# A two-part kernel on one core: block transposes by VectorE and a trip through DRAM in place of TensorE's transposes, with queries cut 64 + 4 x 128

## The chip, the core and the metric

The kernel runs on one NeuronCore of one Trainium2 chip. Its engines run side by side, each with its own queue of instructions worked through in order: TensorE (PE, with its weight loads as PEld), VectorE (DVE), ScalarE (ACT), GpSimd (POOL), and SyncE (SP), which here issues every DMA. The transfers themselves are carried out row by row by 16 DMA engines. The metric is the device time of one execution in microseconds.

## The reference, cut to what matters

```python
# q, k, v: (8 batches, 8 heads, 576, 64), f: (8, 8, 576)
scores = scale * q @ k^T
cum = cumsum(log(clip(f, 1e-4, 1)))                     # over the 576 positions
scores = where(causal, scores + cum[:, None] - cum[None, :], -1e9)
attn = exp(scores - max(scores)); attn /= sum(attn) + 1e-9
x = (attn @ v) transposed and reshaped to (4608, 512)   # one row per token
h = x @ w_in                                            # (4608, 2048)
out = maximum(0.01 * h, h) @ w_out                      # (4608, 512)
```

Everything is float32. The kernel gets this accuracy by splitting a number into a high part (float32r) and a remainder, and by multiplying the parts.

## The kernel before, in words

There are 64 attention tasks, one per head, and behind them one feed-forward layer over 4608 tokens. Batches 3 to 7 are taken whole, which gives 40 tasks with all 576 queries. For batches 0 to 2 the first 256 queries are done in a short "early" phase at the start (`early_load`, `early_scores`, `early_values`), so that their 24 tasks at the end do only queries 256 to 575 (`c0 = 2`). The feed-forward layer runs over groups of 256 tokens; it is cut into small pieces (`ffn`, `second`), which `fill` puts between the attention's pieces, as many per step as the tokens that are ready allow.

One turn of the loop at L694 is a round. In round t the kernel:

- loads q and k of task t + 1 (`load`, L235): each is fetched twice, into partitions 0 to 63 and into 64 to 127, by two DMAs of 64 rows; for each second task the values v of two heads as well;
- computes the scores of task t (`scores`, L403) in five chunks of 128, 128, 128, 96 and 96 queries, each against all keys up to its own end: two matmuls (L420), a mask, scale and row maximum on VectorE (L425), an exponential with its row sum on ScalarE (L431);
- turns the exponentials of task t - 1 (`transposes`, L436): TensorE multiplies each block of 128 keys with an identity (L447) into PSUM, ScalarE writes the high part `ph` (L460) and VectorE the remainder `pl` (L462);
- multiplies them with v (`values`, L474, matmuls on L489) and, when both heads of a pair are done, scales by the inverse row sums. These are turned on TensorE, written to DRAM as `inv` (L515) and read back broadcast over 64 partitions as `rb` (L521, two DMAs of 64 rows); `normalise` (L523) multiplies and writes to `xd` in DRAM, where the feed-forward layer fetches its tokens (L543);
- splits q, k and v of task t + 1 into their parts (`split`, L380), with the high part of q copied to the other half of `s2` by a DMA (L392).

The order within each engine's queue follows a scheduler that works from these calls; within the SP queue a DMA waits for its inputs and its destination, and everything behind it waits too. Eight DMA semaphores are used in turn, so that a DMA also waits for the one eight places ahead of it. The tiles `qraw` and `kraw` have one buffer each: the loads of task t + 2 wait until `split` of task t + 1 has read them.

The lines that the change touches:

Of the kernel before, what the change touches and what calls it, by code (L numbers as in the profile page):

```python
# [23 lines left out]
B2 = 7  # L24
# [9 lines left out]
ZE = (("z0", "z1", "z2", "z3"), ("vm", "s2b", "m2b", "s2a"))  # L34
# [9 lines left out]
def forgetting_attention_ffn(ctx, tc, qT, kT, v4, vr, f, w_in, w_out, out):  # L44
# [15 lines left out]
    STEP = (P + REST) // 2  # L60
    ST = [*range(0, (NFULL - 1) * P + 1, P)]
    ST.append(ST[-1] + STEP)
# [5 lines left out]
    PST = S - P  # L68
    PT0 = NFULL * PST + STEP
    PTW = PT0 + P  # L70
# [7 lines left out]
    def rows(i):  # L78
        return P if i < NFULL - 1 else STEP

    def width(i):
        return ST[i] + rows(i)

# [6 lines left out]

    def segments(n):

        at = n * P
        while at < (n + 1) * P:
            b, lo, hi = next(x for x in reversed(blocks) if place[x[:2]] <= at)
            skip = at - place[b, lo]
            m = min(hi - lo - skip, (n + 1) * P - at)
            yield at - n * P, b * S + lo + skip, m
            at += m

# [31 lines left out]
    inv = dram.tile([NHEAD // 2, 2, S], F32, name="inv")  # L132
    dec_k, dec_q = (dram.tile([NHEAD, 2, S], F32, name=n) for n in ("dec_k", "dec_q"))

    dry = one.tile([P, 1], F32, name="dry")
# [56 lines left out]
    def decays():  # L192
# [42 lines left out]
    def load(t):  # L235
# [4 lines left out]
        for name, src, lo in (("q", qT, a), ("k", kT, 0)):  # L240
            x = h[name] = one.tile([P, S], F32, tag=f"{name}raw", name=f"{name}raw_{t}")
            for o in range(2):
                nc.sync.dma_start(x[o * D:(o + 1) * D, lo:n], src[s][:, lo:n])
        if s % 2 == 0:
# [4 lines left out]
            pairs[s // 2, c0] = dict(vm=vm)  # L249

    early = {}

    def early_load(b, g):

        e = early[b, g] = {}
        x = e["qk"] = one.tile([P, 2, T], F32, tag="b2", name=f"qk_{b}_{g}", bufs=B2)
# [4 lines left out]
        v = e["v"] = one.tile([P, 2, T // P, D], F32, tag="b2", name=f"ve_{b}_{g}", bufs=B2)  # L261
        nc.sync.dma_start(v, v4[b * HPB // 2 + g][:, :, :T // P])

    def early_split(b, g, mx, sm):
# [13 lines left out]
        for i in range(2):  # L278
            n, at = width(i), i * P
# [7 lines left out]
        for i in range(2):  # L287
            n, at = width(i), i * P
            for o in range(2):
                c = 2 * o + i  # L290
                z = e[c] = one.tile([P, n], F32, tag=ZE[g % 2][c], name=f"ze_{b}_{g}_{c}")
# [8 lines left out]
    def early_scores(b, g):  # L300
# [5 lines left out]
        else:  # L306
            for o in range(2):
                s = b * HPB + 2 * g + o
                for i in range(2):
                    n, c = width(i), 2 * o + i  # L310
# [28 lines left out]
    def early_values(b, g):  # L339
        e = early[b, g]  # L340
        out = psum.tile([P, 512], F32, tag="tr", name=f"ave_{b}_{g}")
        for o in range(2):
# [5 lines left out]
            pt = one.tile([P, 3 * P], F32, tag=("z4", "m2a")[o], name=f"pte_{b}_{g}_{o}")  # L348
# [15 lines left out]
    def fix():  # L364

        for x in "ab":
# [4 lines left out]
            y = fixed["sum" + x] = one.tile([P, NCH, 2], F32, tag="sum" + x, name=f"fixed_sum{x}")  # L371
            nc.gpsimd.memset(y, 1.0)
        for i in range(NFULL - 1, NCH):
            z = fixed[f"z{i}"] = one.tile([P, (i + 1) * P], F32, tag=f"z{i}", name=f"fixed_z{i}")
            nc.gpsimd.memset(z, 0.0)
        vs = fixed["vs"] = one.tile([P, 2, NCH, 2 * D], F32R, tag="vs", name="fixed_vs")
        vm = fixed["vm"] = one.tile([P, 2, NCH, D], F32, tag="vm", name="fixed_vm")
        nc.gpsimd.memset(vm[:, :, NFULL], 0.0)

    def split(t):  # L380
# [12 lines left out]
        nc.sync.dma_start(s2[2:4, a:n].bitcast(F32), dec_q[s][:, a:n])  # L393
        nc.sync.dma_start(m2[:2, :n].bitcast(F32), dec_k[s][:, :n])
        minus(s1[:D, a:n], h["q"][:D, a:n], s1[:D, a:n].bitcast(F32))
        minus(m2[D:, :n], h["k"][D:, :n], m1[D:, :n].bitcast(F32))
        p = pairs[s // 2, c0]
        o = s % 2
        vs = fixed["vs"][:, o]
        nc.scalar.copy(vs[:, :, :D], p["vm"][:, o])  # L400
        minus(vs[:, :, D:], p["vm"][:, o], vs[:, :, :D].bitcast(F32))

    def scores(t, i):  # L403
# [3 lines left out]
        m, n = rows(i), width(i)  # L407
        if i < NFULL - 1:
            z = h[f"z{i}"] = one.tile([P, n], F32, tag=f"z{i}", name=f"z{i}_{t}")
        else:  # L410
            z = h[f"z{i}"] = fixed[f"z{i}"]
        z = z[:m, :n]
# [3 lines left out]
        for x, (a, b) in enumerate(parts):  # L416
            ps = psum.tile([P, 512], F32, tag="sc", name=f"sc_{t}_{i}_{x}")
            cols = slice(ST[i], ST[i] + m)
            for y, w in enumerate("12"):
                nc.tensor.matmul(  # L420
                    ps[:m, :b - a], h["s" + w][:, cols], h["m" + w][:, a:b],
                    start=y == 0, stop=y == 1,
                )
            at = TRI - P - ST[i] + a
            nc.vector.tensor_tensor_reduce(  # L425
                out=z[:, a:b], in0=ps[:m, :b - a], in1=tri[:m, at:at + b - a], scale=-SCALE,
# [6 lines left out]
            accum_out=fixed["sum" + "ab"[s // 2 % 2]][:m, i, s % 2:s % 2 + 1],  # L433
        )

    def transposes(t, i):  # L436
        h = state[t]
        if i == tasks[t][1]:
            for w in ("ph", "pl"):
                h[w] = one.tile([P, PTW], F32R, tag=w, name=f"{w}_{t}")  # L440
        m = rows(i)
        z = h[f"z{i}"]
        ps = psum.tile([P, 512], F32, tag="tr", name=f"tr_{t}_{i}")

        blocks_ = [NFULL, *range(NFULL)] if i == NFULL else range(i + 1)
        for x, j in enumerate(blocks_):
            nc.tensor.transpose(  # L447
                ps[:, x * m:(x + 1) * m], z[:m, j * P:(j + 1) * P], ident[:m, :m]
            )
        nblk = len(blocks_)  # L450
        for dst, eng in ((h["ph"], "a"), (h["pl"], "v")):
            if nblk == 1:
                o, hi, src = dst[:, PT0:], h["ph"][:, PT0:], ps[:, :m]
            else:
                first = 0 if i == NFULL else place_p(0, ST[i])
                o = strided(dst, first, nblk, PST, m)
                hi = strided(h["ph"], first, nblk, PST, m)
                src = ps[:, :nblk * m].rearrange("p (j m) -> p j m", m=m)
            if eng == "a":
                nc.scalar.copy(o, src)  # L460
            else:
                nc.vector.tensor_tensor(o, src, hi.bitcast(F32), op=ALU.subtract)  # L462

    def strided(t, start, n, step, m):
        a = t[:, start:start + m]
        return bass.AP(tensor=a.tensor, offset=a.offset, ap=[a.ap[0], [step, n], [1, m]])

    def place_p(j, q):

        if j == NFULL:  # L470
            return q - ST[-1]
        return PT0 + q if q < P else PST * (j + 1) + q - ST[-1]

    def values(t, part):  # L474
# [8 lines left out]
        lo, hi = spans(t)[part]  # L483
        ps = psum.tile([P, 512], F32, tag="tr", name=f"av_{t}_{part}")
        steps = [(w, j) for w in ("ph", "pl") for j in range(NCH) if j * P < hi]
        for n, (w, j) in enumerate(steps):
            a = max(lo, j * P)
            at = place_p(j, a)
            nc.tensor.matmul(  # L489
                ps[:, a - lo:hi - lo], fixed["vs"][:, odd, j, :], h[w][:, at:at + hi - a],  # L490
                start=(n == 0), stop=(n == len(steps) - 1),
# [4 lines left out]
        nc.scalar.copy(y[mine, :hi - lo], ps[other, :hi - lo])  # L496
        nc.vector.tensor_tensor(
# [261 lines left out]
```

## Time and profile before

| what | value |
|---|---|
| three runs | 1196.63, 1197.21, 1198.48 us (median 1197.21) |
| the profiled execution | 1197.86 us, of which the span from first to last instruction is 1196.1 us |
| TensorE, VectorE, ScalarE, GpSimd busy | 99%, 49%, 53%, 36% of the span |
| granted TensorE clock | 1.00 throughout |
| moved by DMA | 110.48 MB, mean 92 GB/s |
| first matmul of the scores of task 0, of task 40, last matmul of `values` | at 128, 836 and 1085 us |

The profile's page gives for each engine its busy time; the chain of waits follows the work back from the last instruction to what released each step; groups collect the instructions of one line and shape; the DMA view counts packets, which are the rows that a DMA engine moves and the 4-byte writes with which it reports to a semaphore. A busy TensorE in this page is one with a matmul somewhere in its pipeline; what a line costs on the path is better read from the chain.

### The profile page before, as it was taken

The numbers are of one execution on the slowest core, as the hardware profiler recorded it, in microseconds if no ns is written. First come the engines' busy times: TensorE is split into PE (matmuls) and PEld (weight loads), VectorE is DVE, ScalarE is ACT, GpSimd is POOL, SyncE is SP. The second block draws the span as 40 slices with busy tenths as digits, with TensorE's granted clock in tenths as the row PEclk, the third lists the DMA queues.
The fourth block names the chain that finished last, engine by engine and source line by source line (L and its number), as shares of the span: only waits on it lengthen the run. The fifth ranks groups of instructions, "written<-read, shape, count | busy, mean of one in ns | idle before, by whom it ended". The sixth has DMA issues, their size and how long they took to land.

```text
span 1196.1 us, 21843 instructions
## 1 busy us (share of the span) xinstructions
PE 1178.5 (99%) x7876; PEld 1050.5 (88%) x7876; DVE 581.3 (49%) x1561; ACT 636.2 (53%) x1531; POOL 436.6 (36%) x347
## 2 busy tenths in 40 slices
PE   9999999999999999999999999999999999999998
PEld 6777888989999989999989999999999899888987
DVE  6888655644545455444454354433343445552221
ACT  7877666755565555555565454433444556652111
POOL 1001534444535344444444443434343444441000
PEclk9999999999999999999999999999999999999999
DMA  7555333333233323333222223122212233321000
GB/s 235 192 182 187 88 118 98 92 115 89 80 99 98 116 68 92 98 106 86 73 87 91 88 67 100 48 76 74 76 55 88 69 101 100 90 69 55 11 18 18
DMA packets 75819, 110.48 MB, mean 92 GB/s; under 512 B 14464, under 2 KB 45424, under 8 KB 75712
## 3 DMA queue, kind: packets, MB, share of 16 engines
q1 hardware_dynamic: 75712, 109.09, 30.4%
q8 instruction: 62, 1.02, 0.3%
q14 instruction: 45, 0.37, 0.1%
HBM read 82.62 MB, written 18.56 MB: 85 GB/s over the span
## 4 chain that ended last, share of the span: by engine, by line
PE 89%; DVE 4%; ACT 3%; issue 2%; POOL 1%; DMA 0%; SPq 0%; DVEq 0%; ACTq 0%; POOLq 0%
PE h L576 32%; PE o L614 31%; PE av L489 8%; PE sc L420 8%; PE tr L447 6%; PE warm L115 1%; DVE wt L170 1%; POOL xs L140 1%; PE ave L351 1%; PE sce L313 1%; ACT ze L296 1%; ACT wt L167 1%; PE tre L345 0%; DVE fixed_z L425 0%; DMA rb<-inv 0%
## 5 line engine op out<-in xcount | busy, mean ns | idle before, releaser
L576 PE MATMUL h<-xh,win_h 128*128 128x256 f32 x1152 | 326.6, 284 | 0.8 <-DVE xh L548 0.8
L576 PE MATMUL h<-xh,win_l 128*128 128x256 f32 x1152 | 323.2, 281 | 0.0
L576 PE MATMUL h<-xs,win_h 128*128 128x256 f32 x1024 | 287.0, 280 | 4.6 <-POOL xs L140 4.6
L140 POOL TENSOR_TENSOR gl<-g,gh 128x512 fp32r<-128x512 f32 x116 | 150.3, 1296 | 319.7 <-DVE gh L589 297.1
L614 PE MATMUL o<-wout_h,gh 128*128 128x512 f32 x576 | 232.8, 404 | 0.0
L614 PE MATMUL o<-wout_l,gh 128*128 128x512 f32 x576 | 229.1, 398 | 0.0
L614 PE MATMUL o<-wout_h,gl 128*128 128x512 f32 x576 | 228.0, 396 | 0.0
L576 PEld LDWEIGHTS h<-xh,win_h 128*128 128x128 f32 x1152 | 217.1, 189 | 7.0 <-DVE xh L548 1.2
L576 PEld LDWEIGHTS h<-xh,win_l 128*128 128x128 f32 x1152 | 216.9, 188 | 0.3 <-issue 0.2
L583 ACT ACTIVATE g<-h 128x512 f32<-128x512 f32 x144 | 85.6, 594 | 220.3 <-PE h L576 219.9
L576 PEld LDWEIGHTS h<-xs,win_h 128*128 128x128 f32 x1024 | 193.0, 188 | 9.9 <-POOL xs L140 6.0
L460 ACT CAST ph<-tr 128x128 fp32r<-128x128 f32 (+2 forms) x272 | 121.7, 449 | 123.5 <-PE tr L447 120.6
L589 DVE CAST gh<-g 128x512 fp32r<-128x512 f32 x144 | 80.2, 557 | 218.1 <-ACT g L583 214.8
L140 POOL TENSOR_TENSOR s<-qraw,s 64x576 fp32r<-64x576 f32 (+1 forms) x64 | 78.9, 1233 | 268.2 <-ACT s L390 264.9
L462 DVE TENSOR_TENSOR pl<-tr,ph 128x128 fp32r<-128x128 f32 (+2 forms) x272 | 138.2, 516 | 42.5 <-ACT ph L460 42.4
L425 DVE CUSTOM_DVE_ANT_0 z<-sc,tri 128x128 f32<-128x128 f32 (+1 forms) x144 | 63.7, 444 | 142.0 <-PE sc L420 141.0
L614 PEld LDWEIGHTS o<-wout_h,gl 128*128 128x128 f32 x576 | 108.4, 188 | 24.6
L614 PEld LDWEIGHTS o<-wout_h,gh 128*128 128x128 f32 x576 | 108.7, 189 | 16.8 <-issue 0.2
L614 PEld LDWEIGHTS o<-wout_l,gh 128*128 128x128 f32 x576 | 108.7, 189 | 15.7
L420 PE MATMUL sc<-m,s 128*128 128x128 f32 (+2 forms) x336 | 121.6, 367 | 0.1
L431 ACT ACTIVATE fixed_z<-fixed_z,max 96x480 f32<-96x480 f32 (+1 forms) x128 | 94.3, 737 | 43.8 <-DVE max L425 42.5
L425 DVE CUSTOM_DVE_ANT_0 fixed_z<-sc,tri 96x480 f32<-96x480 f32 (+1 forms) x128 | 70.4, 550 | 75.9 <-PE sc L420 75.1
(129 smaller groups left out, 1826.5 us busy)
## 6 DMA issues: line engine op xcount, KB each, us to landing
kraw<-in_kT SPq DMA_DIRECT2D x128, 144.0 KB
qraw<-in_qT SPq DMA_DIRECT2D x80, 144.0 KB
wraw<-in_w_in SPq DMA_DIRECT2D x16, 512.0 KB
wraw<-in_w_out SPq DMA_DIRECT2D x16, 512.0 KB
fixed_vm<-in_v SPq DMA_DIRECT2D x32, 256.0 KB
xs<-xd SPq DMA_DIRECT2D x16, 512.0 KB
out<-ost SPq DMA_DIRECT2D x28, 256.0 KB
rb<-inv SPq DMA_DIRECT2D x40, 144.0 KB
```

The costliest lines, as they stand in the source:

```text
L140: nc.gpsimd.tensor_tensor(out, a, b, op=ALU.subtract)
L420: nc.tensor.matmul(ps[:m, :b - a], h["s" + w][:, cols], h["m" + w][:, a:b], start=y == 0, stop=y == 1,)
L425: nc.vector.tensor_tensor_reduce(out=z[:, a:b], in0=ps[:m, :b - a], in1=tri[:m, at:at + b - a], scale=-SCALE, scalar=3.0e38 if x == 0 else ...
L431: nc.scalar.activation(z, z, AF.Exp, bias=h["max"][:m, last:last + 1], scale=-1.0, accum_out=fixed["sum" + "ab"[s // 2 % 2]][:m, i, s % 2: ...
L447: nc.tensor.transpose(ps[:, x * m:(x + 1) * m], z[:m, j * P:(j + 1) * P], ident[:m, :m])
L460: nc.scalar.copy(o, src)
L462: nc.vector.tensor_tensor(o, src, hi.bitcast(F32), op=ALU.subtract)
L489: nc.tensor.matmul(ps[:, a - lo:hi - lo], fixed["vs"][:, odd, j, :], h[w][:, at:at + hi - a], start=(n == 0), stop=(n == len(steps) - 1),)
L576: nc.tensor.matmul(ph[:, e, :], w[:, c, fs], xx[:, c, :], start=(c == 0 and x == 0), stop=(c == NCC - 1 and x == 2),)
L583: nc.scalar.activation(g, ph, AF.Prelu, alpha=0.01)
L589: nc.vector.tensor_copy(gh, g)
L614: nc.tensor.matmul(acc[k], gg[:, e, ts], w[:, e, :], start=(fc_ == 2 * p0 and x == 0), stop=(fc_ == 2 * p1 - 1 and x == 2),)
```

## The change

Queries are cut into chunks of 64, 128, 128, 128 and 128. The exponentials z (queries on partitions) are no longer turned by TensorE. `turn` lets VectorE transpose them in blocks of 32 by 32 inside each group of 32 partitions, into a tile `zt`. What is still missing is that blocks change their group of partitions; for that `send` writes `zt` to DRAM (`zd`) and `receive` reads it back with another order of partitions into `pl`. `divide` then makes the high part `ph` on ScalarE and the remainder in place on VectorE, both from SBUF. `values` multiplies as before, in one part of 512 queries and one of 64, with its operands read in runs of 32 and so with queries, and in the end tokens, in a permuted order; the writes to `out` undo it in pieces of 32 rows.

The trip takes a round: values of task t - 2 are computed in round t. `load` now fetches q and k by one DMA each, whose source has a leading dimension of 2 with step 0; `rb` is read in the same manner by one DMA. `receive` uses four DMAs, each with a source of 4 by 32 rows. ScalarE copies the high part of q into `s2` in place of the DMA. The tile `zt` takes SBUF from other tiles (B2 goes from 7 to 5, the early phase uses other tiles).

```diff
-B2 = 7
+B2 = 5
-    ST = [*range(0, (NFULL - 1) * P + 1, P)]
-    ST.append(ST[-1] + STEP)
+    ST = [0, *range(REST, S, P)]
+    Q = 32
+    FW, PW = 15 * Q, 12 * Q
...
+    zd = [dram.tile([4, P, FW], F32, name=f"zd_{x}") for x in range(2)]
...
             x = h[name] = one.tile([P, S], F32, tag=f"{name}raw", name=f"{name}raw_{t}")
-            for o in range(2):
-                nc.sync.dma_start(x[o * D:(o + 1) * D, lo:n], src[s][:, lo:n])
+            y = src[s][:, lo:n]
+            y = bass.AP(tensor=y.tensor, offset=y.offset, ap=[[0, 2], *y.ap])
+            nc.sync.dma_start(x[:, lo:n], y)
...
+        nc.scalar.copy(s2[D:, a:n], h["q"][D:, a:n])
...
-        nc.sync.dma_start(s2[D:, a:n].bitcast(F32), s1[D:, a:n].bitcast(F32))
...
-    def transposes(t, i):
...
-            nc.tensor.transpose(
-                ps[:, x * m:(x + 1) * m], z[:m, j * P:(j + 1) * P], ident[:m, :m]
-            )
...
+    def turn(t, i):
...
+            nc.vector.transpose(
+                ap(zt[0][:m], base + u * Q, *dims), z[:, js[0] * P:(js[-1] + 1) * P]
             )
...
+        nc.vector.transpose(ap(zt[0][:m], base + u * Q, [w, 2]), z[:, i * P:i * P + 2 * Q])
+
+    def send(t, part):
...
+        to = zd[t % 2][:, :, lo:hi].rearrange("b p c -> p b c")
+        nc.sync.dma_start(to, src.rearrange("p (b c) -> p b c", b=4))
+
+    def receive(t):
+
+        w = PW if tasks[t][1] else FW
+        zq = state[t]["pl"] = one.tile([P, 4 * FW], F32R, tag="pl", name=f"pl_{t}")
+        for a in range(4):
+            y = zd[t % 2][:, a * Q:(a + 1) * Q, :w]
+            nc.sync.dma_start(zq[:, a * w:(a + 1) * w].bitcast(F32), y)
+
+    def divide(t, half):
...
+        nc.scalar.copy(ph, z.bitcast(F32))
+        nc.vector.tensor_tensor(z, z.bitcast(F32), ph.bitcast(F32), op=ALU.subtract)
...
-        for o in range(2):
-            src = inv[s // 2, o, a:n]
-            src = bass.AP(tensor=src.tensor, offset=src.offset, ap=[[0, D], *src.ap])
-            nc.sync.dma_start(rb[o * D:(o + 1) * D, a:n], src)
+        y = inv[s // 2, :, :m * P]
+        y = bass.AP(tensor=y.tensor, offset=y.offset, ap=[y.ap[0], [0, D], y.ap[1]])
+        nc.sync.dma_start(rb[:, :m * P], y)
...
+                for x, row, m, times, far in segments(n * T // P + k):
+                    y = out[row:row + m, :]
+                    if times > 1:
+                        y = bass.AP(tensor=y.tensor, offset=y.offset, ap=[[far * DM, times], *y.ap])
+                    nc.sync.dma_start(y, o[x:x + m * times])
...
         for i in range(5):
-            if i in before:
-                transposes(t - 1, i)
+            if i == 0 and 0 < t <= nt:
+                spread(t - 1, 4)
             if i in now:
                 scores(t, i)
+            if i - 1 in now:
+                spread(t, i - 1)
+            if old is not None and i in (1, 2):
+                divide(old, i - 1)
             fill(step)
...
+            if old is not None and i == 3:
+                values(old, 0)
...
+                if 0 < t <= nt:
+                    receive(t - 1)
```

(`old` is t - 2; `spread` calls `turn`, and `send` once the first three and once all five chunks of a task are turned.)

The queue of SP in the middle of the whole tasks, before: a destination tile, its source, the size of the destination, and in brackets what the DMA waits for (DMAHW0 to 7 are the eight DMA semaphores). From one task's loads to the next, with the inverse sums of a pair between them:

```order
L243 DMA qraw_4391<-in_qT 64x576 [waits DMAHW6_49,Pool_49]
L243 DMA qraw_4391<-in_qT 64x576 [waits DMAHW7_49]
L243 DMA kraw_4394<-in_kT 64x576 [waits DMAHW0_49,Pool_49]
L243 DMA kraw_4394<-in_kT 64x576 [waits DMAHW1_49]
L394 DMA fixed_m2b<-dec_k 2x576 [waits DMAHW2_49]
L515 DMA inv<-rt_4438 3x2x128 [waits DMAHW3_49,Activation_49]
L515 DMA inv<-rt_4438 2x2x96 [waits DMAHW4_49]
L521 DMA rb_4442<-inv 64x576 [waits DMAHW5_49,DMAHW4_49,DMAHW3_49]
L521 DMA rb_4442<-inv 64x576 [waits DMAHW6_49]
```

The same place in the changed kernel, from the reading back of one task (`pl` from `zd`, four DMAs) to that of the next:

```order
L537 DMA pl_2772<-zd_128 128x1x480 [waits DMAHW1_49,DMAHW2_49,DVE_49,PE_49]
L537 DMA pl_2772<-zd_128 128x1x480 x3
L272 DMA qraw_2804<-in_qT 128x1x576 [waits DMAHW5_49,Pool_49]
L272 DMA kraw_2806<-in_kT 128x1x576 [waits DMAHW6_49,Pool_49]
L529 DMA zd_127<-zt 128x4x288 [waits DMAHW7_49,DVE_49]
L426 DMA fixed_s2a<-dec_q 2x576 [waits DMAHW0_49]
L427 DMA fixed_m2a<-dec_k 2x576 [waits DMAHW1_49]
L529 DMA zd_128<-zt 128x4x192 [waits DMAHW3_49,DMAHW4_49,DMAHW2_49,DVE_49]
L537 DMA pl_2911<-zd_127 128x1x480 [waits DMAHW7_49,DVE_49,PE_49]
```

The loads of q and k are one DMA each with 128 rows in the destination, and they stand between the reading of one `pl` and the second `send` (288 columns) of the task whose `pl` is read next.

The queue of TensorE in a round before (the transposes of chunks 3 and 4 of one task, the scores of the same chunks of the next):

```order
L447 MATMUL tr_3_4470<-ident_r,fixed_z_1543 128x96 x4
L420 MATMUL sc_3_0_4477<-m_16_4363,s_16_4362 96x480
L420 MATMUL sc_3_0_4477<-fixed_m2a,fixed_s2a 96x480
L447 MATMUL tr_4_4482<-ident_r,fixed_z_1545 128x96 x5
L420 MATMUL sc_4_0_4490<-m_16_4363,s_16_4362 96x288
L420 MATMUL sc_4_0_4490<-fixed_m2a,fixed_s2a 96x288
```

In the changed kernel the rows of L447 are gone, and the scores stand between the matmuls of the feed-forward layer alone:

```order
L465 MATMUL sc_2_0_3390<-m_12_3292,s_12_3291 128x320 [waits DVE_49]
L465 MATMUL sc_2_0_3390<-fixed_m2a,fixed_s2a 128x320
L670 MATMUL h_1_3362<-xh_3054,win_h_94 128x256
L670 MATMUL h_1_3362<-xs_2955,win_h_94 128x256
L670 MATMUL h_1_3362<-xh_3054,win_l_102 128x256
```

More of the change, by code (lines that the diff above doesn't have):

```diff
@@ L89, in forgetting_attention_ffn, with tokens @@
         total += hi - lo
+    def tokens(lo, hi):
+        if hi - lo == T:
+            return [(0, T)]
+        first = 0 if lo == 0 else 2
+        runs = [(0, REST)] if lo == 0 else []
+        for a in range(P // Q):
+            for c in range(max(first, 1), NCH):
+                at, m = max(ST[c], lo), width(c) - max(ST[c], lo)
+                if a * Q < m:
+                    runs.append((at + a * Q, Q))
+        return runs
+    where = []
+    for b, lo, hi in blocks:
+        for at, m in tokens(lo, hi):
+            where += range(b * S + at, b * S + at + m)
     def segments(n):
-        at = n * P
+        runs, at = [], n * P
         while at < (n + 1) * P:
[L95 to L98, printed above, removed]
+            m = 1
+            while at + m < (n + 1) * P and where[at + m] == where[at] + m:
+                m += 1
+            runs.append([at - n * P, where[at], m, 1, 0])
             at += m
+        merged = []
+        for x, row, m, _, _ in runs:
+            p = merged[-1] if merged else None
+            if p and p[2] == m and p[3] * m + p[0] == x and row > p[1] and (p[3] == 1 or row - p[1] == p[3] * p[4]):
+                p[4] = row - p[1] if p[3] == 1 else p[4]
+                p[3] += 1
+            else:
+                merged.append([x, row, m, 1, 0])
+        return [p for p in merged]
     one = ctx.enter_context(tc.tile_pool(name="one", bufs=1))
@@ L347, in early_values @@
                 )
[L348 removed]
+            if o:
+                pt = one.tile([P, 3 * P], F32, tag="m2a", name=f"pte_{b}_{g}_{o}")
+            else:
+                pt = zt[0][:, 12 * P:]
             nc.scalar.copy(pt, ps[:, :3 * P])
@@ L406, in scores @@
         h = state[t]
[L407 to L412, printed above, removed]
+        m, n, at = rows(t, i), width(i), begin(t, i)
+        z = h[f"z{i}"] = one.tile([P, n], F32, tag="z" + "ab"[i % 2], name=f"z{i}_{t}")
+        z = z[:m]
         if i == c0:
@@ L432, in scores @@
             z, z, AF.Exp, bias=h["max"][:m, last:last + 1], scale=-1.0,
-            accum_out=fixed["sum" + "ab"[s // 2 % 2]][:m, i, s % 2:s % 2 + 1],
+            accum_out=fixed["sum" + "ab"[s // 2 % 2]][:m, s % 2, i:i + 1],
         )
-    def transposes(t, i):
-        h = state[t]
[L438 to L447, printed above, removed]
-                ps[:, x * m:(x + 1) * m], z[:m, j * P:(j + 1) * P], ident[:m, :m]
-            )
[L450 to L462, printed above, removed]
@@ L474, in values @@
+    def divide(t, half):
+        h = state[t]
+        w = 2 * (PW if tasks[t][1] else FW)
+        if not half:
+            h["ph"] = one.tile([P, 4 * FW], F32R, tag="ph", name=f"ph_{t}")
+        c = slice(half * w, (half + 1) * w)
+        z, ph = h["pl"][:, c], h["ph"][:, c]
+        nc.scalar.copy(ph, z.bitcast(F32))
+        nc.vector.tensor_tensor(z, z.bitcast(F32), ph.bitcast(F32), op=ALU.subtract)
     def values(t, part):
@@ L692, in forgetting_attention_ffn, with spread @@
     load(0)
+    prepare(0)
     split(0)
-    for t in range(nt + 1):
+    def spread(t, i):
+        if tasks[t][1] and not tasks[t - 1][1] and i == 2:
+            nc.gpsimd.memset(zt[0][:, :4 * PW], 0.0)
+        turn(t, i)
+        if i == 4 or i == 2 and not tasks[t][1]:
+            send(t, i // 4)
+    for t in range(nt + 2):
         if t + 1 < nt:
             load(t + 1)
-        before = list(range(*tasks[t - 1][1:])) if t else []
+        if t < nt:
+            load_v(t)
         now = list(range(*tasks[t][1:])) if t < nt else []
+        old = t - 2 if t > 1 else None
         have = ready[0] // T * NQ - used[0]
-        left = min((e + 2 - t for e in ends if e + 1 >= t), default=1)
+        left = min((e + 3 - t for e in ends if e + 2 >= t), default=1)
         step = min(have / (left + SLACK), MAXQ) / 8
```

225 lines of the change are left out of this document (140 added, 85 removed).

## The prediction

> **What bounds the kernel now.** I read the busy shares first, then the chain of waits, which says what each line costs on the path.
>
> ```profile
> PE 1178.5 (99%) x7876; PEld 1050.5 (88%) x7876; DVE 581.3 (49%) x1561; ACT 636.2 (53%) x1531; POOL 436.6 (36%) x347
> by line: PE h L576 31.9%; PE o L614 31.0%; PE av L489 7.9%; PE sc L420 7.9%; PE tr L447 6.4%; issue 1.6%; PE warm L115 1.2%; DVE wt L170 0.8%; POOL xs L140 0.8%; PE ave L351 0.8%; PE sce L313 0.7%; ACT ze L296 0.7%; ACT wt L167 0.5%; PE tre
> ```
>
> TensorE is the bound: the two feed-forward lines, the matmuls of `values` (av), the scores (sc) and the transposes (tr) hold 85% of the chain. The other engines and the transfers have room on average. Next the stages: head, whole tasks, late tasks, and feed-forward alone (columns: stage, its us, busy us of PE, PEld, DVE, ACT, POOL, granted clock, share of the 16 DMA engines, GB/s).
>
> ```profile
> 0.00:128.00 128.00, 122.38 (x719) 92.32 (x720) 101.47 (x244) 97.64 (x225) 13.89 (x26) 1.00 0.58 192
> 128.00:836.00 708.00, 703.05 (x4797) 640.28 (x4795) 343.86 (x972) 390.77 (x974) 309.31 (x230) 1.00 0.31 90
> 836.00:1085.00 249.00, 247.00 (x1695) 223.26 (x1694) 113.67 (x306) 133.09 (x309) 108.60 (x90) 1.00 0.27 78
> 1085.00:1196.00 111.00, 106.11 (x671) 94.62 (x669) 22.35 (x40) 14.69 (x25) 4.76 (x2) 1.00 0.08 27
> ```
>
> A round takes 708/40 = 17.7 us for a whole task and 249/24 = 10.4 us for a late one; TensorE is idle for 7 us in 957.
>
> **The gain on TensorE.** All 888 transposes go (15 in each of 40 whole tasks, 12 in each of 24 late ones): 6.4% of 1196.1 = 76.6 us. av and sc are 7.9% = 94.5 us each, and I scale them by the columns that stream through. av: a whole task has 2 x (448 + 448 + 320 + 192 + 64 + 128) = 3200 columns, then 2 x (512 + 512 + 384 + 256 + 128 + 64) = 3712; a late one 2432, then 3072; with 40 and 24 tasks 186,368 become 222,208, or +18.1 us. sc: 2 x 1824 become 2 x 1600, and 2 x 1440 become 2 x 1344; 215,040 become 192,512, or -9.9 us. The sum is -68.4 us. That TensorE reads in runs of 32 with steps between is not in the trace; I take it as free, and 18 us more would be the price of a fifth on av.
>
> **What stands beside other work.** VectorE loses `pl` from PSUM (138.2 us) and gains two subtractions of 960 (or 768) columns a task and the block transposes of 113,664 columns in all.
>
> ```profile
> L462 DVE TENSOR_TENSOR pl<-tr,ph 128x128 fp32r<-128x128 f32 (+2 forms) x272 | 138.2, 516 | 42.5 <-ACT ph L460 42.4
> L589 DVE CAST gh<-g 128x512 fp32r<-128x512 f32 x144 | 80.2, 557 | 218.1 <-ACT g L583 214.8
> L530 DVE TENSOR_TENSOR x<-x,rb 128x576 f32<-128x576 f32 x20 | 22.8, 1142 | 2.4 <-DMA rb<-inv 1.7
> ```
>
> By the cast (1.09 ns a column) and the product from SBUF (1.98 ns) the transposes cost 124 to 225 us, and the subtractions, again 113,664 columns, as much each. VectorE comes to 581 - 138 + 248 to 450 = 691 to 893 us, below the 1129 us that TensorE would need; I take neither as a bound. ScalarE's `ph` and copy of q, and the split buffers (B2 of 5), replace or add some tens of us on engines half idle: nothing on the path.
>
> **The transfers: where this change is decided.** The trip moves 128 x 1920 x 4 bytes = 983 KB out and 983 KB back for a whole task, 786 KB each way for a late one; with the DMA of q's high part gone, 109 MB become 218.6 MB. Against the whole page that looks harmless:
>
> ```profile
> DMA packets 75819, 110.48 MB, mean 92 GB/s; under 512 B 14464, under 2 KB 45424, under 8 KB 75712
> q1 hardware_dynamic: 75712, 109.09, 30.4%
> ```
>
> Twice 30.4% of the 16 engines, over a shorter run, is some 65%. But that holds only if each transfer spreads over all 16. The DMA view of three short stretches shows how they spread, because each engine that takes part ends its share with a 4-byte write to the semaphore, a packet of its own. First 600 to 604 us, two writes of `out`; then 605 to 605.9, one load of 2 rows (`s2` from `dec_q`); then 616 to 618, the two writes of `inv`:
>
> ```profile
> GB/s 0 0 0 0 0 0 0 20 348 389 348 389 369 471 246 41 0 0 0 0 0 0 0 0 0 0 0 0 143 389 369 451 369 369 389 144 0 0 0 0
> DMA packets 288, 0.52 MB, mean 131 GB/s; under 512 B 32, under 2 KB 32, under 8 KB 288
> q1 hardware_dynamic: 288, 0.52, 34.7%
> ...
> DMA packets 4, 0.00 MB, mean 5 GB/s; under 512 B 2, under 2 KB 2, under 8 KB 4
> ...
> DMA packets 15, 0.00 MB, mean 2 GB/s; under 512 B 9, under 2 KB 15, under 8 KB 15
> ```
>
> Two times 128 rows leave 288 - 256 = 32 short packets: 16 engines each. The load of 2 rows leaves 2. The `inv` writes have 6 rows of 512 B and 4 of 384 B, so 5 of the 15 packets are reports. One of them has leading dimensions 3 (DRAM side) and 6 (SBUF side), the other 2 and 4: 3 + 2 = 5 engines, not 6 + 4. The run's total confirms it, with the counts of issues:
>
> ```profile
> fixed_vm<-in_vr SPq DMA_DIRECT2D x32, 32.0 KB
> ...
> inv<-rt SPq DMA_DIRECT2D x32, 3.0 KB
> inv<-rt SPq DMA_DIRECT2D x32, 1.5 KB
> ```
>
> Of the 14,464 packets under 512 B, 32 x 128 = 4096 are the 256-byte rows of v's rest and 32 x 4 the 384-byte rows of `inv`; the other 10,240 are 614 wide DMAs x 16, 128 loads of 2 rows x 2, and 32 x (3 + 2). So a DMA is cut along the leading dimension only, in as many parts as both sides allow: the 6 rows of one side weren't cut in 6, since the other side leads with 3.
>
> The new loads of q and k lead with 2 on the source side and 128 on the other: **2 engines**. So does `rb`. `pl` leads with 4: **4 engines**. Most pieces of `out` lead with 2. In the old kernel each of these led with 64 or 128.
>
> The Trainium skill has this as a rule ("DMA: Bandwidth & Descriptors", section "Why a DMA increments its semaphore by 16 and not by 1"): the number of engines is the largest up to 16 that divides the slowest dimension of both sides; its rules for authors name a leading broadcast with step 0 as the case to avoid. The trace agrees in its 192 narrow DMAs, but has none with a wide destination and a narrow source, where "the destination alone decides" would read the same; by the rule the sum is the one below, without it that of the first rival.
>
> **What a narrow transfer costs.** In 600 to 604 us the two `out` writes took 34.7% of 16 x 4.0 us = 22.2 us of engine time for 524 KB: 23.6 KB/us on one engine. The dearer end is 608 to 611 us, where q and k are loaded (0.58 MB):
>
> ```profile
> q1 hardware_dynamic: 317, 0.58, 66.3%
> ```
>
> 66.3% of 48 us is 31.8 us: 18.2 KB/us, with four DMAs of 64 partitions and all engines at once. I take 23.6, since two or four engines get in each other's way less than 16. On engines 0 and 1 (whichever two they are) a whole task then costs:
>
> - q and k: 2 x 128 rows x 2304 B / 2 = 295 KB: 12.5 us
> - `pl`: 983 KB / 4 = 246 KB: 10.4 us
> - `rb`: 128 x 2560 B / 2 for a pair, 82 KB a task: 3.5 us
> - `zd`: 983 KB / 16: 2.6 us; `out`, mostly in 2s: 42 KB, 1.8 us; v, `xs`, `xd`: 28 KB, 1.2 us
>
> That is **32.0 us**, against 17.7 us for the whole round now. A late task: q 3.5, k 6.25, `pl` 8.3, `rb` 2.1, `zd` 2.1, `out` 1.8, rest 1.0: **25.0 us**, against 10.4. Together 40 x 32.0 + 24 x 25.0 = 1880 us.
>
> Can it be hidden? No: it is a throughput, not a latency. All DMAs stand in one queue, and the engines work it off in order. By the rows of SP above the ring goes: `pl`, q and k of the task after next, second part of `zd`, `pl` of the next task, which waits for that `zd`. Its landing lies behind q and k on these two engines; between landing and the next `pl` I put 1 us of idle (0 to 3), 64 us in all. Split, scores and block transposes of a task run beside the next `pl` and q, k (some 22 us) and do not lengthen it. TensorE then waits behind scores whose `split` hasn't come, and its 68 us gained are idle time.
>
> **The sum.** Head 128 us (its loads are wide) + 1880 + 64 + one more stage at the end (the last `pl` and its values, 10 us) + feed-forward alone 111 us = 2193 us of span; the profiled execution was 1197.86 us beside 1196.1 of span, so add 1.8: **2195 us**, against that 1197.86 and the median of 1197.21.
>
> **The rivals.**
> - *The destination's leading dimension alone decides*, so that q, k, `rb` and `pl` run on 16 engines. The narrow rows above fit that too (their destinations lead with 2 and 3). Against it stands that a source of 2 or 4 blocks would then be cut below its leading dimension, and at `inv` a side of 3 x 2 rows wasn't cut so, though 6 engines could have taken a row each. It decides everything: the busiest engine then has some 32.0 - 12.5 - 10.4 - 3.5 + (590 + 983 + 164 KB) / 16 / 23.6 = 10 us a round, under TensorE's 16, and the time is 1197.9 - 68.4 = **1130 us**, faster. Chance 0.10.
> - *Narrow, but on other engines each time.* Then the load evens out to about 10 us a round and engine, and only latency grows (12.5 us for q and k, under a round). Between 1130 and 1250 us, say **1190**. Chance 0.03. (The Trainium skill, "DMA: Bandwidth & Descriptors", same section, speaks against it: it has such a DMA on the lowest-numbered engines; no row here names an engine.)
> - *Narrow, at the dear rate.* 1880 x 23.6 / 18.2 = 2438, with the rest of the sum **2753 us**. For it: most loads of q and k in the trace ran so; against: there 16 engines were at it. Chance 0.06.
>
> **How the numbers follow.** The forecast has 0.81. Its own range goes from no idle at a rate of 24.3 KB/us (389 GB/s over 16, as in the full tenths of us of those `out` writes), 1826 + 251 = 2077, with 4% off for rows that overlap on an engine, 1990 us, to 2500, about half way to the dear rate. The rivals outside it hold 0.19, so the range stays there. Slower by over 0.2%: 0.81 + 0.06 + half of the second rival, 0.88; faster 0.11; within 0.2%, which is about what a measurement of this kernel tells from no change, 0.01.
>
> **What would show it.** Rounds of 32 us (first scores of one task to those of the next), TensorE busy for little over half the span and waiting at the scores for `split`, and behind it for the DMAs of `qraw` and `kraw`; an average DMA share that falls (about 26%) although twice the bytes move: the sign of few engines. The count of short packets tells the first step apart from the rest: 8,256 short rows and 7,214 reports if both sides decide, 12,526 reports if the destination does. If `tr` is gone, rounds are 16 us and TensorE is at 99%, the step on the leading dimension is wrong and nothing else in the sum matters.

## The result and the profile after

| | before | after |
|---|---|---|
| median of four runs | 1196.92 us (1196.33 to 1198.48) | 2170.96 us (2168.16 to 2171.43) |
| profiled span | 1196.1 us | 2166.4 us |
| ratio after to before | | 1.813 (95% interval 1.810 to 1.816) |

The page of the changed kernel: busy time of the engines, granted clock of TensorE and mean share of the 16 DMA engines in 40 slices (in tenths), packets, the one DMA queue that carries the kernel's transfers, and the chain by engine and by line.

```profile
PE 1373.4 (63%) x6988; PEld 1176.0 (54%) x6988; DVE 720.7 (33%) x2046; ACT 667.5 (31%) x1451; POOL 427.1 (20%) x346
...
PEclk9987766677787777777787787788888877767799
DMA  7523222233232222233223222323233222323100
...
DMA packets 158556, 220.01 MB, mean 102 GB/s; under 512 B 15470, under 2 KB 130718, under 8 KB 158446
...
q1 hardware_dynamic: 158446, 218.65, 29.3%
...
DMA 62%; PE 13%; SPq 10%; DVE 5%; ACT 4%; issue 4%; POOL 1%; ACTq 0%; POOLq 0%; DVEq 0%
DMA zd<-zt 20%; DMA pl<-zd 16%; DMA qraw<-in_qT 16%; SPq L537 6%; DMA inv<-rt 5%; PE o L708 4%; PE h L670 4%; DMA kraw<-in_kT 3%; PE av L581 2%; DMA fixed_vm<-in_vr 1%; PE sc L465 1%; DVE z L470 1%; ACT ph L547 1%; ACT z L476 1%; SPq L272 1%
```

TensorE held 85% of the chain with five lines and now holds 13% in all; transfers hold 62%. Yet the queue's share of the engines' time is 29.3%, a little under the 30.4% of before, for twice the bytes. By slices the DMA share stays at two to three tenths from the head to the end. It is a mean over 16 engines. The short packets say how many engines that is: 15,470, which is 8,256 short rows plus the 7,214 reports of the forecast, and not the 12,526 reports of its first rival.

TensorE's waits in the changed kernel (its line, what it waited for: us in total, times, longest):

```profile
PE sc L465 <- DVE max L470: 388.3, 81, 15.1
PE av L581 <- ACT ph L547: 146.1, 24, 13.7
PE o L708 <- DVE gh L683: 48.2, 9, 13.9
```

The names are VectorE's and ScalarE's, which are busy for a third of the time. They stand in the middle of a chain. The costliest groups there show what they waited for in turn (busy us, mean ns of one | idle us before, with its releasers):

```profile
L548 DVE TENSOR_TENSOR pl<-pl,ph 128x960 fp32r<-128x960 f32 (+1 forms) x128 | 141.7, 1107 | 574.9 <-ACT ph L547 574.9
...
L515 DVE STREAM_TRANSPOSE zt<-z 128x128 f32<-128x128 f32 (+2 forms) x336 | 129.2, 406 | 398.6 <-DMA zd<-zt 273.4 <-ACT z L476 96.5 <-ACT g L677 9.5
L547 ACT CAST ph<-pl 128x960 fp32r<-128x960 f32 (+1 forms) x128 | 119.3, 932 | 619.9 <-DMA pl<-zd 619.9
...
L519 DVE STREAM_TRANSPOSE zt<-z 64x64 f32<-64x64 f32 (+1 forms) x272 | 56.8, 209 | 132.9 <-ACT z L476 101.0 <-DMA zd<-zt 31.6
```

VectorE waited to overwrite `zt` until `zd` had been written, ScalarE for `pl`. Both releasers are DMAs. One round of the chain (start us, us, what):

```profile
588.31 18.11 DMA zd<-zt
...
608.25 10.85 DMA pl<-zd
...
628.17 6.35 DMA inv<-rt
...
641.20 12.92 DMA pl<-zd
```

`zd` is a wide transfer, some 1.6 us of work for each of 16 engines, and takes 18.11 us. The DMA view of two pieces of this round, first 590 to 594 us, then 613 to 617 us (packets; the queue's packets, MB and share of 16 engines; the DMA issued there):

```profile
DMA packets 104, 0.21 MB, mean 51 GB/s; under 512 B 4, under 2 KB 70, under 8 KB 104
...
q1 hardware_dynamic: 104, 0.21, 13.2%
...
zd<-zt SPq DMA_DIRECT2D x1, 576.0 KB
...
DMA packets 218, 0.40 MB, mean 101 GB/s; under 512 B 8, under 2 KB 218, under 8 KB 218
...
q1 hardware_dynamic: 218, 0.40, 26.1%
```

13.2% of 16 is 2.1 engines, 26.1% is 4.2 (rows overlap a little): the loads of q and k, then the reading of `pl`. 51 GB/s over 2.1 engines is 24.3 KB/us each, 101 over 4.2 is 24.0. The `zd` that the chain names was being issued in the first piece, in SP's queue (start us, us, line, DMA):

```profile
588.31 7.37 SPq L529 DMA_DIRECT2D zd<-zt  x1
```

Two things make its 18.11 us. The issue itself held SP for 7.37 us (a `zd` of e5 below takes 0.53 on average). Then 448 of its 512 rows, the share of 14 engines, ran from 596.2 to 599.1 us; the last 64, 32 on each of two engines, ran only from 604 to 605.9, when the rows of q and k were through. So the wide transfer waited on the engines that q and k use. SP's issuing took 1346 us in all, beside 417 before. What holds an issue isn't shown, but the sum falls as narrow transfers are widened: 967 us in e3, 799 in e2, 632 in e5. Counted over the whole trace, exactly two rows of SP's queue are in flight for 753 us, exactly four for 516 us, and none for 206 us.

### The profile page after: what moved, and what is told of

It reads as the page before. It is cut to its first block, busy times and chain, and to the rows that moved or that the text cites. A ratio compares the mean times of both kernels' runs of the same rounds, so it can differ in the third digit from the quotient of the medians.

```text
span 2166.4 us, 21113 instructions
## 1 busy us (share of the span) xinstructions
PE 1373.4 (63%) x6988; PEld 1176.0 (54%) x6988; DVE 720.7 (33%) x2046; ACT 667.5 (31%) x1451; POOL 427.1 (20%) x346
## 2 busy tenths in 40 slices
DMA packets 158556, 220.01 MB, mean 102 GB/s; under 512 B 15470, under 2 KB 130718, under 8 KB 158446
## 3 DMA queue, kind: packets, MB, share of 16 engines
q1 hardware_dynamic: 158446, 218.65, 29.3%
## 4 chain that ended last, share of the span: by engine, by line
DMA 62%; PE 13%; SPq 10%; DVE 5%; ACT 4%; issue 4%; POOL 1%; ACTq 0%; POOLq 0%; DVEq 0%
DMA zd<-zt 20%; DMA pl<-zd 16%; DMA qraw<-in_qT 16%; SPq L537 6%; DMA inv<-rt 5%; PE o L708 4%; PE h L670 4%; DMA kraw<-in_kT 3%; PE av L581 2%; DMA fixed_vm<-in_vr 1%; PE sc L465 1%; DVE z L470 1%; ACT ph L547 1%; ACT z L476 1%; SPq L272 1%
## 5 line engine op out<-in xcount | busy, mean ns | idle before, releaser
L465 PE MATMUL sc<-m,s 128*128 128x64 f32 (+2 forms) x336 | 138.7, 418 | 475.3 <-DVE max L470 388.3
L465 PEld LDWEIGHTS sc<-m,s 128*128 128x128 f32 x336 | 78.4, 235 | 516.3 <-DVE max L470 400.7
L548 DVE TENSOR_TENSOR pl<-pl,ph 128x960 fp32r<-128x960 f32 (+1 forms) x128 | 141.7, 1107 | 574.9 <-ACT ph L547 574.9
L547 ACT CAST ph<-pl 128x960 fp32r<-128x960 f32 (+1 forms) x128 | 119.3, 932 | 619.9 <-DMA pl<-zd 619.9
L708 PE MATMUL o<-wout_h,gl 128*128 128x512 f32 x576 | 260.4, 452 | 4.7 <-POOL gl L168 4.6
L515 DVE STREAM_TRANSPOSE zt<-z 128x128 f32<-128x128 f32 (+2 forms) x336 | 129.2, 406 | 398.6 <-DMA zd<-zt 273.4
L476 ACT ACTIVATE z<-z,max 64x64 f32<-64x64 f32 (+4 forms) x272 | 160.1, 589 | 273.3 <-DVE max L470 271.4
L581 PE MATMUL av<-ph,fixed_vs 128*128 128x512 f32 (+3 forms) x360 | 98.6, 410 | 161.7 <-ACT ph L547 146.1
L581 PEld LDWEIGHTS av<-ph,fixed_vs 128*128 128x128 f32 x360 | 88.5, 264 | 181.4 <-ACT ph L547 155.5
L470 DVE CUSTOM_DVE_ANT_0 z<-sc,tri 64x64 f32<-64x64 f32 (+4 forms) x272 | 116.7, 434 | 30.5 <-PE sc L465 26.8
```

The source lines that it names most:

```text
L465: nc.tensor.matmul(ps[:, :b - a], h["s" + w][:, cols], h["m" + w][:, a:b], start=y == 0, stop=y == 1,)
L470: nc.vector.tensor_tensor_reduce(out=z[:, a:b], in0=ps[:m, :b - a], in1=tri[:m, u:u + b - a], scale=-SCALE, scalar=3.0e38 if x == 0 else h ...
L476: nc.scalar.activation(z, z, AF.Exp, bias=h["max"][:m, last:last + 1], scale=-1.0, accum_out=fixed["sum" + "ab"[s // 2 % 2]][:m, s % 2, i: ...
L515: nc.vector.transpose(ap(zt[0][:m], base + u * Q, *dims), z[:, js[0] * P:(js[-1] + 1) * P])
L547: nc.scalar.copy(ph, z.bitcast(F32))
L548: nc.vector.tensor_tensor(z, z.bitcast(F32), ph.bitcast(F32), op=ALU.subtract)
```

## The experiments

"Engine work" below is the forecast's table with an edit put in: KB on the busiest engine over 23.6 KB/us. Rounds are read from the traces: first scores of task 0 to those of task 40 over 40, and from there to the last matmul of `values` over 26 (24 late tasks and two rounds behind them; 25 in the old kernel, where `values` lags by one).

**e1, e2, e3: one narrow transfer made wider.** In e1 and e2 q and k are read by two DMAs of 64 rows again; e1's source is put in an order that leads with 4, e2's as before the change:

```diff
-            y = bass.AP(tensor=y.tensor, offset=y.offset, ap=[[0, 2], *y.ap])
-            nc.sync.dma_start(x[:, lo:n], y)
+            y = bass.AP(tensor=y.tensor, offset=y.offset, ap=[[S, 4], [4 * S, D // 4], [1, n - lo]])  # e1 only
+            for o in range(2):
+                nc.sync.dma_start(x[o * D:(o + 1) * D, lo:n], y)
```

e3 leaves q and k at 2 engines and lets the source of `pl` lead with its 32 rows in place of its 4 blocks; v is laid out to match in its inputs:

```diff
-            y = zd[t % 2][:, a * Q:(a + 1) * Q, :w]
+            y = zd[t % 2][:, a * Q:(a + 1) * Q, :w].rearrange("b r c -> r b c")
```

> q and k are loaded by two DMAs each of 64 rows whose source leads with 4 instead of one whose source leads with 2 (the 64 dimensions of a head are taken in another order, the same for q and k). Theory (work of the two busiest DMA engines): 12.5 us a whole task become 6.25 on four engines, the round 25.8 us, a late one 20.1; 366 us off 2171: about 1805 us, and 7,982 short reports instead of 7,214. Rival 1 (the latency of one task's way through DRAM sets the round, not the work of the engines): within 50 us of 2171. Rival 2 (the bytes of the trip load the memory or all engines): unchanged.

> As e1, but the two DMAs of 64 rows lead with 64 on both sides, as in the kernel before. Theory: q and k cost 1.6 us a whole task on each engine instead of 12.5, the round is 21.1 us, a late one 16.4; 642 us off 2171: about 1530 us. With e1 the time then falls with the number of engines, at the same number of DMAs. Rival 1 (latency of the way through DRAM): above 2050. Rival 2 (bytes): unchanged.

> Only the reading back of the exponentials is changed: the source's two outer dimensions are exchanged, so that it leads with 32 instead of 4 (keys lie in another order on the partitions, and v is laid out to match, its rest of 64 keys repeated to 128 rows that meet zeros). Number and size of the DMAs stay. Theory: pl costs 2.6 us a whole task on each engine instead of 10.4, 2.1 instead of 8.3 in a late one: rounds of 24.2 and 18.8 us, 461 us off 2171: about 1710 us. Rival 1 (latency): also about 1700, since the same us leave the chain. Rival 2 (bytes): unchanged, the same bytes move.

Measured: e1 1870.76 us, e2 1785.50, e3 1805.43, one run each (as are e4, e10 and e11 below). The packet rows of e1, e2 and e3, in that order:

```profile
DMA packets 159324, 220.01 MB, mean 118 GB/s; under 512 B 16238, under 2 KB 131486, under 8 KB 159214
```
```profile
DMA packets 162397, 220.02 MB, mean 123 GB/s; under 512 B 19311, under 2 KB 134559, under 8 KB 162287
```
```profile
DMA packets 165725, 221.07 MB, mean 123 GB/s; under 512 B 22639, under 2 KB 137887, under 8 KB 165615
```

Each grows by what "the leading dimension of both sides" asks for. e1: 256 DMAs with 4 reports in place of 128 with 2, +768. e2: with 16, +3840. e3: 256 DMAs with 16 in place of 4, +3072, and 4096 more rows of v's rest. The counts fit to the packet; e2 and e3 have one more on the page, which isn't in SP's queue. e1 and e2 have the same DMAs and bytes and differ only in the order of a source: the number of engines alone is worth 85 us there, and the step from 2 to 4 (with two DMAs in place of one) 300 us.

All three ran longer than expected. By rounds (us; whole task, late task):

| | engine work | measured round |
|---|---|---|
| after | 32.0, 25.0 | 31.1, 25.4 |
| e1: q, k on 4 | 25.7, 20.1 | 26.4, 21.7 |
| e3: `pl` on 16 | 24.2, 18.8 | 25.3, 20.4 |
| e2: q, k on 16 | 21.1, 16.5 | 24.9, 20.8 |

While the fullest engine has 24 us or more to do, it sets the round to within 1.1 us in the whole tasks. At 21 it no longer does. Two rounds of e2's chain (start us, us, what):

```profile
608.27 12.26 DMA qraw<-in_qT
620.55 3.82 DMA inv<-rt
...
626.30 13.76 DMA pl<-zd
...
648.53 9.56 DMA zd<-zt
...
660.62 12.70 DMA qraw<-in_qT
```

Four landings, one behind the other, are 39.4 of 52.4 us. The load of q, now 0.8 us of work on each engine, lands after 12.26 us, since the rows of `pl` stand ahead of it on four engines: 192 of the 256 rows of q and k are through by 615 us, and the last 64, the share of four engines, run from 619 us on, when the last rows of `pl` do. And `pl` isn't issued again before a `zd` has landed.

**e10, e11: q and k in another queue.** If the place behind `pl` in SP's queue is what q pays for, ScalarE's queue should free it (e10, else as e2). e11 does the same to the changed kernel and leaves q and k at two engines.

```diff
-                nc.sync.dma_start(x[o * D:(o + 1) * D, lo:n], src[s][:, lo:n])
+                nc.scalar.dma_start(x[o * D:(o + 1) * D, lo:n], src[s][:, lo:n])
```

> e2 (q and k loaded wide) with these four DMAs a task issued by ScalarE, so that they have a queue of their own and needn't stand behind pl, which still runs on four engines. e2 came out 256 us slower than the work of the busiest engines gives. Theory A (in e2 the wide loads wait in the same queue behind the 10 us of pl, and the round is that chain of landings): 1600 to 1700 us instead of 1786. Theory B (an engine does one packet at a time whatever queue it is from, so that the loads still wait, or something else sets e2's round): within 50 us of 1786.

> The changed kernel with nothing but the issuer of the loads of q and k changed, from SP to ScalarE; they still run on two engines each. Theory (work of the two busiest engines): these engines have the same work, so within 70 us of 2171. Rival 1 (the order in SP's queue sets the round): 1950 or less. Rival 2 (another issuer means other engines): about 1700, as if q and k were off the engines that pl uses.

e10: 1737.80 us, 48 less than e2: at the very edge (50) of what the second theory allowed, and 38 above the first's range. The chain by line, e2 and then e10:

```profile
DMA pl<-zd 35%; DMA qraw<-in_qT 9%; SPq L536 8%; PE av L580 7%; PE o L707 6%; PE h L669 5%; DMA inv<-rt 4%; ACT ph L546 2%; PE sc L464 1%; DMA zd<-zt 1%; PE warm L142 1%; SPq L726 1%; DVE x L587 1%; PE ave L390 1%; SPq L607 1%
```
```profile
DMA pl<-zd 41%; SPq L536 6%; PE o L707 6%; PE av L580 6%; DMA zd<-zt 5%; PE h L669 5%; DMA inv<-rt 2%; ACT ph L546 2%; PE sc L464 2%; DMA xd<-x 1%; DMA kraw<-in_kT 1%; DMA qraw<-in_qT 1%; DMA rb<-inv 1%; DVE z L469 1%; ACT z L475 1%
```

The wait for q goes from 9% to 1%, and `pl` on its four engines takes its place. So `pl`, the second narrow transfer, seems to bound e2 (e5 tests that), and with 10.4 us of work in a round of 24.9 more by its landing than by its throughput; how much of the rest (24.0 us a round in e10 against 21.1 of engine work) is the handing over from `zd` to `pl`, and how much TensorE at its lower clock, stays open.

e11: 2263.22 us, 92 more than the changed kernel and 22 above the upper end expected. Both ways of gaining are out: q and k don't run beside SP's transfers on engines of their own. The Trainium skill ("DMA: Bandwidth & Descriptors", section "Issuing engines are not separate DMA queues") says that transfers of all issuers share the same 16 engines; the run agrees, with a loss in place of a gain. The chain has `pl` at 32% in place of 16%; where the 92 us come from stays open.

**e4: the narrow loads alone, in the old kernel.** The two loops of 64 rows at L243 become one DMA that leads with 2, as in the change; nothing else.

> The kernel before with one edit of the change: q and k loaded by one DMA each with a leading 2 and step 0 in the source; no trip through DRAM, TensorE still transposes. Theory: the two busiest engines get 15.5 us a whole task (under the round of 17.7, hidden) and 12 us a late one (over the 10.4): 24 x 1.6 = 38 us and something for the later splits: 1200 to 1260 us. Rival 1 and 2 (the trip through DRAM is what costs): 1197 or a little less, since 128 DMAs fewer are issued.

Measured: 1289.25 us beside 1196.91, 7.7% slower and 29 us above the expected range. Its page:

```profile
DMA packets 71978, 110.45 MB, mean 86 GB/s; under 512 B 10624, under 2 KB 41584, under 8 KB 71872
...
DMA kraw<-in_kT 34%; PE h L577 17%; PE o L615 17%; PE sc L421 4%; PE av L490 3%; PE tr L448 3%; POOL fixed_m2a L140 2%; ACT fixed_z L432 1%; PE warm L115 1%; ACT m L392 1%; DMA fixed_s2b<-s 1%; ACT ze L297 1%; DVE gh L590 1%; PE ave L352 1%; DMA out<-part 1%
```

10,624 short packets are 3840 fewer than the 14,464 of before: two reports for each of 128 DMAs, sixteen for 256. The load of k, which wasn't on the chain, holds 34% of it. Without any trip, this one edit costs 92 us. The work of the two engines alone doesn't give that: rounds grew from 16.0 and 12.8 us to 17.2 and 14.1, over the 15.5 and 12 of engine work in the expectation. That expectation also took the old rounds for 17.7 and 10.4 us (the next section has that cut). How the loss divides between landing and work isn't shown.

**e5: all the narrow transfers widened.** e2 and e3 together, and `rb` by two DMAs of 64 rows.

> e2 and e3 together, and rb read by two DMAs of 64 rows: every large transfer but the pieces of out leads with 32 or more on both sides. Theory as it stands after e1 to e3 (work of the busiest engines, and what queues behind a narrow transfer on them): both go, each engine has some 10 us of work in a whole round, TensorE is the bound again and the sum on TensorE holds: 1197 - 68 = 1130 us, up to 1160 with what the longer way of a task and 160 more DMAs on SP leave. Rival (the way through DRAM keeps its own latency or its bytes cost): well above 1197, 1400 or more by the steps that e2 and e3 made. 15,086 short reports.

Measured: 1269.56 us (1268.06 to 1275.24), 1.0605 of before (1.0587 to 1.0623). Its page:

```profile
PE 1158.3 (91%) x6988; PEld 1005.2 (79%) x6988; DVE 753.0 (59%) x2046; ACT 664.1 (52%) x1451; POOL 440.5 (35%) x346
...
DMA packets 170524, 221.09 MB, mean 174 GB/s; under 512 B 27438, under 2 KB 142686, under 8 KB 170414
...
q1 hardware_dynamic: 170414, 219.73, 56.2%
...
PE 45%; DMA 19%; DVE 9%; SPq 9%; ACT 8%; issue 7%; POOL 3%; ACTq 0%; DVEq 0%; POOLq 0%
```

Nearly the same bytes, and 901 of the 974 us are gone, far more than the rival allowed. But it isn't the 1130 to 1160 us expected. The DMA share is 56%, now that 16 engines are in use; 73 us over before remain, with TensorE at 91% and not 99%.

**e6, e7, e8, e12: is the rest SP's queue?** The longest waits in e5's SP queue (line, what it waited for: us, times, longest) are the write of `out` and the write of `xd`:

```profile
SPq L727 <- ACT ost L722: 97.5, 9, 41.8
SPq L630 <- DVE x L629: 80.0, 14, 11.1
```

e6 issues `out` from ScalarE; e7 `xd` too; e8 is e6 with q and k; e12 has all three. Each edit is of the form

```diff
-                    nc.sync.dma_start(y, o[x:x + m * times])
+                    nc.scalar.dma_start(y, o[x:x + m * times])
```

> e5 with the pieces of out issued by ScalarE right behind its copy of them, instead of SP, where loads stand behind a piece that waits for that copy (97 us of waits of SP in e5). Theory A (in e5 the single queue of SP holds loads back behind DMAs that wait): 30 to 80 us off 1270, 1190 to 1240. Theory B (the landing times along one round, zd to pl to q and k, set the round whoever issues): within 15 us of 1270.

> e6 with the writes of xd also issued by ScalarE (113 us of waits of SP in e5 stand before them). Theory A: below e6, 1160 to 1200. Theory B: as e6. Against both: ScalarE may now wait for VectorE's product before xd and hold its own exponentials.

> e6 with the loads of q and k also issued by ScalarE, which reads these tiles itself. Theory A: below e6, 1150 to 1200, at the price of some 2.4 us a round of ScalarE. Theory B: 1250 or more.

> e7 and e8 together: all large transfers wide, and out, xd, q and k issued by ScalarE. If what is left over the kernel before comes from the order in SP's queue: 1190 to 1230, below e7's 1244. If it comes from TensorE waiting for the longer chain of VectorE (scores, block transposes, remainders), as in e9 without the trip: 1235 to 1260.

Measured, beside before: e6 1275.66 (1.0658, 1.0627 to 1.0689), e7 1243.69 (1.0391, 1.0357 to 1.0424), e8 1259.59 (1.0523, 1.0493 to 1.0554), e12 1274.14 (1.0644, 1.0613 to 1.0675). The longest wait, for `ost`, cost nothing: with it moved away the time is no lower (6 us more, with e5's own runs up to 1275.24). `xd` was worth 32 us, q and k 16 us; but both together lose it all. So e6 and e8 came as Theory B had it, e7 as neither, and e12 above both of its ranges. In e12 TensorE waits longer for `ph` than in e7. Its waits, of e7 and then of e12:

```profile
PE av L580 <- ACT ph L546: 12.9, 6, 6.1
```
```profile
PE av L580 <- ACT ph L546: 33.1, 21, 5.2
```

ScalarE computes `ph`, and that is the likeliest reading: what SP no longer waits for, ScalarE does. It isn't shown: TensorE's wait for VectorE's `max` falls from 35.1 to 20.1 us between the same two runs. No version that computes all of it came below before.

**e9: no trip.** With q, k and `rb` wide, `send` and `receive` do nothing, and `divide` takes its input from `zt`, so that the kernel leaves out the last step of the transposition:

```diff
-        nc.scalar.copy(ph, z.bitcast(F32))
-        nc.vector.tensor_tensor(z, z.bitcast(F32), ph.bitcast(F32), op=ALU.subtract)
+        nc.scalar.copy(ph, zt[0][:, c])
+        nc.vector.tensor_tensor(z, zt[0][:, c], ph.bitcast(F32), op=ALU.subtract)
```

> The kernel with q, k and rb loaded wide (as e2, and rb as in e5) and without the way through DRAM: divide reads zt where it stands, so that exponentials of other blocks and tasks are multiplied with v; send and receive are left out. TensorE, VectorE and ScalarE do the same work. The sum of the prediction on TensorE (-68 us, block transposes and the copy of q hidden): 1130 us, 1115 to 1150. If VectorE or ScalarE has become a bound: above 1170.

Measured: 1192.03 us, 0.9954 of before (0.9928 to 0.9981), on the side of the rival. So the trip costs 78 us even with wide transfers (e5 less e9), and the rest of the change, freed from it, is worth 5 us and not 68. Which part of the trip costs the 78 us stays open. e9 also has a tie that e5 lacks: `ph` is read straight from `zt`, and ScalarE waits 82 us for that, so that with a trip that cost nothing the kernel might still be faster than e9. TensorE's waits in e9:

```profile
PE sc L464 <- DVE max L469: 23.7, 19, 5.9
PE sc L464 <- POOL fixed_m2a L168: 13.2, 13, 1.5
PE sc L464 <- POOL fixed_m2b L168: 5.2, 8, 1.2
```

In before none of these three is in the list, whose largest entry is 4.6 us.

## Why the forecast came out, step by step

The 974 us lost are, by these runs, 901 from narrow transfers (after less e5) and 78 from the trip with wide ones, less 5 from all else.

- **The cut along the leading dimension of both sides: shown.** Counts to the packet, over the kernel's own transfers, in every kernel here (in e5, 3840 + 3072 + 4096 + 960 for `rb` more than in the changed kernel, 27,438), two and four busy engines in the trace, and a dose: q and k on 2, 4, 16 engines are 2171, 1871, 1786 us. The rivals fall by it: a wide destination doesn't help, and neither q and k nor `pl` goes to free engines: the last 64 rows of `zd` wait on two engines for q and k, and those of q and k in e2 on four for `pl`.
- **The rate: near, some 7% too low.** 24.0 to 24.3 KB/us of engine time against 23.6 taken. Since rows overlap a little on an engine, 51 GB/s on two engines and 101 on four are 25.5 and 25.3 KB/us each over the time that passed. The dear rate of 18.2 doesn't show where only two or four engines work; in e5, with 16, it nearly does: 219.73 MB in 56.2% of 16 x 1273.5 us is 19.2.
- **The sum: right, with errors that cancel.** Cut at the first scores of task 0 and of task 40 and at the last matmul of `values` (columns as in the stages of before):

```profile
138.00:1383.00 1245.00, 730.57 (x3530) 628.38 (x3529) 402.08 (x1236) 369.03 (x814) 261.10 (x199) 0.75 0.29 103
1383.00:2043.00 660.00, 406.81 (x2053) 355.31 (x2052) 194.88 (x526) 184.87 (x385) 145.81 (x121) 0.77 0.28 98
2043.00:2166.00 123.00, 111.71 (x701) 100.24 (x700) 23.68 (x42) 15.36 (x26) 4.81 (x2) 0.96 0.08 24
```

  The whole tasks took 1245 us against 40 x 33.0 = 1320, the late ones and what stands behind them 660 against 24 x 26.0 + 10 = 634. The head is 11 us longer than forecast, as q and k of the first task are narrow too (130 us in e2), and the end 12 us. That -75 and +49 leave only -26 in 2193 us is luck in part. What was too high is the work: 32.0 x 23.6 / 25.4 is 29.7 us. The 1 us of idle a round holds: in the whole tasks no row of SP's queue is in flight for 1.2 us a round.
- **A cut of before that was off.** The stages in the prediction and the table of before divide at 836 us, which isn't where task 40 begins. Its first scores are at 766 us:

```profile
128.00:766.00 638.00, 633.05 (x4325) 576.33 (x4324) 318.10 (x906) 361.03 (x907) 279.29 (x207) 1.00 0.31 91
766.00:1085.00 319.00, 317.00 (x2166) 287.20 (x2164) 139.43 (x372) 162.82 (x376) 138.62 (x114) 1.00 0.27 78
```

  A round of before takes 16.0 and, over 25, 12.8 us, and not 17.7 and 10.4. No term of the sum came from these; the comparison with them did, and so did the range expected of e4.
- **VectorE: sizes right, "nothing on the path" right only here.** The transposes took 129.2 + 56.8 = 186.0 us (124 to 225 forecast), the subtractions 141.7, VectorE in all 720.7 (691 to 893). Under the transfers that is free. In e9, where they are gone, scores wait 23.7 us for VectorE and 18.4 for GpSimd, which splits k (part of it perhaps by e9's own tie).
- **TensorE's gain: nearly right in size, gone as forecast, and not there for the taking.** From start to start of its matmuls (300 ns of each at most; the rest counted as idle), e9 against before: transposes -63.5 (-76.6 forecast), scores -9.2 (-9.9), `values` +13.5 (+18.1), feed-forward +2.9, in all -56.3 us against -68.4. Idle time rises by 42.3 us. The first rival's 1130 us was therefore some 60 too low, by e9, even where no trip is in the way.
- **The signs.** Rounds of 31.1 us, scores that wait behind DMAs and the count of short packets came as forecast. The DMA share is 29.3% and not 26%. TensorE is busy for 63%, more than "little over half", and that has a cause of its own, below.

## What to carry to other kernels

Before one DMA takes the place of two, look at the outermost dimension that is left on each side: a broadcast of 2 written as a leading step of 0 leaves two engines of sixteen, and in the old kernel that edit alone cost 92 us. Such a queue looks idle on a page of the profile that averages over 16 engines, and the chain names the wide transfers stuck behind the narrow ones; count the reports to the semaphores, and multiply the DMA share of a short stretch by 16. And a step that is free under one bound is not free under the next: take the bound away in a run before counting on the gain behind it.

## What the hardware showed beyond that

- **TensorE got slower as it got idler.** The granted clock was 1.00 throughout before, and 0.78 after: 103 stretches of 3.4 to 27.3 us at half clock, 956 us in all. In the feed-forward layer's first half, a matmul of `xh` with `win_h` takes 309 ns on average in place of 284, and TensorE's busy time rose from 1178.5 to 1373.4 us though 888 transposes left. The Trainium skill ("TensorE: Matmul & The Clock Gate", section "Part 1: The HAM clock gate (the "warmup" mystery)") gives a half clock after at least one idle window of about 3.4 us. The length agrees (stretches come in steps of 3.4 us), the idleness only in part: in the 3.4 us right ahead of the 103 stretches TensorE was busy for 0 to 56% of the time, 18% in the median. Where two engines set the round, as here, that can have cost little; in e2, whose rounds hang on latency (clock 0.82 in its whole tasks), it may be part of what stayed open.
- **Nearly the same bytes take more engine time with more engines at work**: 10,157 us (29.3% of 16 x 2166.4) for 218.65 MB in the changed kernel, 11,451 us for 219.73 MB in e5. A row of 2304 bytes, the size of q's and k's, takes 98 ns on average in the changed kernel and 125 in e5.
